# Two constant tables made on the chip from short rows, and two loads in another order

## The chip, the cores and the metric

The kernel runs on one core of one Trainium2 chip. The metric is the device time of one execution in microseconds (us); times are compared by their medians. A core has five engines that run side by side, each through its own queue in order: TensorE (PE in the rows, and PEld for its weight loads), VectorE (DVE), ScalarE (ACT), GpSimd (POOL) and SyncE (SP), which here only issues the loads and stores.

## The reference

Three stages. The first is a decayed linear attention ("retention") over 2 batches, 8 heads, 768 positions, 64 columns; each head has its own decay gamma:

```python
gamma = 1.0 - 2.0 ** (-5.0 - np.arange(H, dtype=np.float32))
for t in range(S):
    state = gamma[None, :, None, None] * state + np.einsum('bhd,bhe->bhde', k[:, :, t], v[:, :, t])
    y[:, :, t] = scale * np.einsum('bhd,bhde->bhe', q[:, :, t], state)
```

Its output, 1536 tokens of 512 columns, goes through two MLPs of width 2048: softplus between the two products of the first, `s * relu(h)**2 + b` between those of the second. Everything is float32.

## The kernel before

**The retention.** Each batch is cut into six chunks of 128 positions, twelve chunks in all; a chunk is done in two *units* of four heads, so unit n is half n % 2 of chunk n // 2. Before a unit stand its *scores* (`att_scores`, line 172: the products of k and q, eight passes on PE) and the *mask* (`att_mask`, line 179: VectorE multiplies the scores by a table). The unit itself (`att_out`, line 191) is, on PE, the product of state and scaled q (not in a batch's first chunk), the product of masked scores and v, and the product of k and scaled v that updates the state. ScalarE and VectorE then take the result out in two parts (`x_hi`, `x_lo`, lines 223 and 229), add up the state (`state`, lines 244 and 246), copy it to where PE reads it (`state_out`, line 255) and decay it (`decay`, line 262). GpSimd makes the scaled v and q of the next chunk (`scale_v`, line 145; `scale_q`, line 157).

**The tables.** They stand in one tile `cst`: `vtab` (128 x 8, decays for v), `gam` (128 x 4, decays for the state), `mask` (128 x 1024: for each head a 128 x 128 triangle of decay powers, divided by the square root of 64) and `gtab` (128 x 512: decay powers for q). All are computed on the host by `_constants` and loaded in two loads, at lines 729 (`vtab`, `gam`, `mask`) and 731 (`gtab`). The masks of scores 0 and 1 need the first, `scale_q(1)` the second.

**The order.** Everything is in an order written out by hand. All loads are issued by SP, one after another, at lines 728 to 738: q and k of chunk 0 (`load_qk`), the mask table, k and v of chunk 0 (`load_kv`), the query table, then q, k and v of the next chunks; `load_next` loads the next 512 KB of MLP weights. Every load of q and k, of k and v, and of weights has 512 KB. Later loads are issued as buffers come free (lines 677 to 680 and 755 to 757).

PE's queue begins with *fill-in products* of zeros that compute nothing (`warm`, line 742): six ahead of score 0 ("first"), three between score 1 and unit 0 ("u0"), one after unit 1 ("s2"). Each is a float32 product of 128 x 128 by 128 columns and shows as two passes. Then come scores 0 and 1, unit 0, unit 1, scores 2 and 3, unit 2, score 4, unit 3, score 5, unit 4, score 6, and so on (line 760). Between the units, `fill` puts steps of the splitting of weights (`split_w`, lines 288 to 303) on VectorE and ScalarE, from unit 3 on.

From unit 8 on, the first MLP's products (`h_mm`, line 354; `acc_mm`, line 405) stand between the units; after the last unit the rest of both MLPs follows, products of 512 columns on PE with the splitting of weights and values into two parts beside them. PSUM banks `ac[2]` and `ac[3]` and the result tiles `xa[0]` and `xa[1]` are free while the retention starts.

Of the kernel before, what the change touches and what calls it, by code (L numbers as in the profile page):

```python
# [10 lines left out]
AF = mybir.ActivationFunctionType  # L11
ALU = mybir.AluOpType

P = 128
B, H, S, D = 2, 8, 768, 64
DM = H * D
DFF = 2048
NT = B * S
C = 128
NC_B = S // C  # L20
NP = H // 2
# [7 lines left out]
RING = 6  # L29
NIN = 4  # L30

WARM = {"first": 6, "u0": 3, "s2": 1}
FIRST, SECOND = (0, 1), (2, 3)
LAG = 3
LAG_U = 3
# [1 line left out]
HF = 2  # L37
HP = NP // HF
# [4 lines left out]
CM = H + NP  # L43
CG = CM + H * C
CW = CG + NP * C


@with_exitstack
def tile_retention_mlps(ctx: ExitStack, tc: tile.TileContext, head, w1, w2, sb, out):
    nc = tc.nc  # L50
# [18 lines left out]
    def bank(pool, tag):  # L69
        return pool.tile([P, 512], F32, tag=tag, name=tag)  # L70

    def sums():

        t = ps_acc.tile([P, 2, 512], F32, tag="acc01", name="acc01")
        return [t[:, 0], t[:, 1], bank(ps_acc, "acc2"), bank(ps_acc, "acc3")], t

    cst = rp.tile([P, CW], F32, tag="cst", name="cst")
    vtab = cst[:, 0:H]
    gam = cst[:, H:CM]
    mask = cst[:, CM:CG].rearrange("p (f h t) -> p f h t", f=HF, h=2)  # L80
    gtab = cst[:, CG:]
# [10 lines left out]
    xa = [cp.tile([P, KC, TT], F32, tag=f"xa{j}", name=f"xa{j}") for j in range(NTILE)]  # L92
# [7 lines left out]
    ac, ac01 = sums()  # L100
# [18 lines left out]
    NCHUNK = B * NC_B  # L119
    NU = NCHUNK * HF  # L120

    consts = head[: P * CW].rearrange("(p x) -> p x", p=P)

    def chunk_of(k):
        at_ = P * (CW + 2 * DM * k)
        return head[at_ : at_ + P * 2 * DM].rearrange("(p x) -> p x", p=P)

    def load_qk(ci):
        t = qk_t[ci] = inp.tile([P, 2, NP, C], F32, tag="qk", name="qk")
        nc.sync.dma_start(out=t.rearrange("p a b t -> p (a b t)"), in_=chunk_of(2 * ci))  # L130

    def load_kv(ci):
        t = kv_t[ci] = inp.tile([P, 2, DM], F32, tag="kv", name="kv")
        nc.sync.dma_start(out=t.rearrange("p a b -> p (a b)"), in_=chunk_of(2 * ci + 1))

    def scale_v(ci):

        if ci % NC_B == NC_B - 1:
            return
        t = scp.tile([P, H, D], F32, tag="v2", name="v2")  # L140
        v = kv_t[ci][:, 1].rearrange("p (h d) -> p h d", h=H)
        vs = vtab.rearrange("p (h o) -> p h o", o=1).to_broadcast([P, H, D])
        cuts = (0, H // 2, H) if ci == 0 else (0, H)
        for a, z in zip(cuts, cuts[1:]):
            nc.gpsimd.tensor_tensor(out=t[:, a:z], in0=v[:, a:z], in1=vs[:, a:z], op=ALU.mult)
        v2_t[ci] = t

    def scale_q(ci):

        if ci % NC_B == 0:  # L150
            return
        t = scp.tile([P, NP, C], F32, tag="q2", name="q2")
        flat = "p a t -> p (a t)"

        cuts = (0, NP // 2, NP) if ci == 1 else (0, NP)
        for a, z in zip(cuts, cuts[1:]):
            nc.gpsimd.tensor_tensor(
                out=t[:, a:z].rearrange(flat), in0=qk_t[ci][:, 0, a:z].rearrange(flat),
                in1=gtab[:, a * C : z * C], op=ALU.mult,
            )  # L160
        q2_t[ci] = t
# [107 lines left out]
    def load_w(w, i):  # L269
        layer, f = divmod(w, NF)  # L270
        t = rawp.tile([P, DM, 2], U32, tag="raw", name="raw")
        nc.sync.dma_start(out=t.rearrange("p a b -> p (a b)"), in_=(w1, w2)[layer][f, :, i].bitcast(U32))
        raw_t[w, i] = t
# [358 lines left out]
    def load_next():  # L632
        x = next(loads, None)
        if x:
            load_w(*x)
# [20 lines left out]
    def unit(n, y, before=lambda: None, mid=lambda: None):  # L656

        att_out(n, y)
        before()
        x_hi(n)  # L660
        mid()
        if n == 1:
            state_out(0)
        if n < N0:
            decay(n - 1)
        state(n)
        if n > 0:
            state_out(n)
        if n >= N0:
            decay(n - 1)  # L670
        x_lo(n)
        ci, f = divmod(n, HF)
        if f == 0 and ci + 1 < NCHUNK:
            scale_q(ci + 1)
            scale_v(ci + 1)
        if f == HF - 1 and ci + NIN < NCHUNK:
            load_qk(ci + NIN)
            if ci == 0:
                load_next()
            load_kv(ci + NIN)  # L680

    def score_to(n, banks):
        while scored[0] < min(n, NU):
            n_, scored[0] = scored[0], scored[0] + 1
            att_scores(n_, banks(n_))
            att_mask(n_, banks(n_))
# [17 lines left out]
    def out_of(y):  # L704
        return y[:, :HC], y[:, HC : HC + HP * D]
# [3 lines left out]
    def fill(n):  # L709

        for _ in range(n):
            if not left[0]:
                if nxt[0] is None or fill.at < slot_free(*nxt[0]):
                    return
                work[0] = split_w(*nxt[0])
                nxt[0] = next(splits, None)
                left[0] = 5
            next(work[0], None)
            left[0] -= 1

    with tc.manual_schedule():
# [3 lines left out]
        nc.vector.memset(st, 0.0)  # L725
        nc.vector.memset(cu[:, 0:1], 0xC0000000)
        nc.vector.memset(cu[:, 1:2], 29)
        load_qk(0)
        nc.sync.dma_start(out=cst[:, :CG], in_=consts[:, :CG])
        load_kv(0)  # L730
        nc.sync.dma_start(out=cst[:, CG:], in_=consts[:, CG:])
        load_qk(1)
        load_kv(1)
        load_qk(2)
        load_next()
        load_kv(2)
        load_qk(3)
        load_kv(3)

        def warm(bank, key):  # L740
            for _ in range(WARM[key]):
                nc.tensor.matmul(bank[:, 0:P], zero[:, 0:P], zero[:, P : 2 * P], start=True, stop=True)

        ys = [bank(ps_h, "h"), bank(ps_y, "y")]
        warm(ac[3], "first")
        scale_q(0)
        scale_v(0)
        score_to(2, lent)
        warm(ac[3], "u0")
        for n in range(N0):  # L750
            if n >= len(ys):
                ys.append(bank(*((ps_h, "h"), (ps_y, "y"))[n % 2]))
            unit(n, out_of(ys[n]))
            if n == 1:
                load_next()
                load_next()
                nc.sync.dma_start(out=sbt, in_=sb)
                warm(ac[3], "s2")

            score_to((2, 4, 5, 6, 7, 8, 9, 10)[n], lent)  # L760
            fill((0, 0, 0, 2, 1, 1, 2, 2)[n])
# [289 lines left out]
        for s in range(S1, NS):  # L1051
            k = s - S1
# [23 lines left out]
        p = PAIRS - 1  # L1076
        for j in (1, 2):
            cuts = (FIRST, SECOND) if j == 1 else (FIRST, SECOND[:1], SECOND[1:])
# [7 lines left out]


def _constants():
    import numpy as np

    gamma = 1.0 - 2.0 ** (-5.0 - np.arange(H, dtype=np.float64))
    t = np.arange(C, dtype=np.float64)
    of = 2 * np.arange(NP)[None, :] + (np.arange(P) >= D)[:, None]
    gap = t[None, :] - t[:, None]

    mask = np.where(gap[:, None] >= 0, gamma[:, None] ** np.maximum(gap, 0)[:, None], 0) / np.sqrt(D)
    mask = mask.reshape(P, HF, HP, 2, C).transpose(0, 1, 3, 2, 4).reshape(P, H * C)
    gtab = gamma[of][:, :, None] ** (t + 1.0)[None, None, :] / np.sqrt(D)
    vtab = gamma[None, :] ** (C - 1.0 - t)[:, None]
    gam = gamma[of] ** C  # L1100
    return np.ascontiguousarray(
        np.concatenate([vtab, gam, mask, gtab.reshape(P, NP * C)], axis=1).astype(np.float32)
    )


def _layout(x):

    v = x.reshape(B, NP, 2, NC_B, C, D)
    return v.transpose(0, 3, 2, 5, 1, 4).reshape(B, NC_B, P, NP, C)


def _natural(x):

    return x.reshape(B, H, NC_B, C, D).transpose(0, 2, 3, 1, 4).reshape(B, NC_B, C, DM)


def _head(q, k, v):

    import numpy as np

    qk = np.stack([_layout(q), _layout(k)], axis=3).reshape(B * NC_B, 1, -1)
    kv = np.stack([_natural(k), _natural(v)], axis=3).reshape(B * NC_B, 1, -1)
    return np.concatenate([_constants().reshape(-1), np.concatenate([qk, kv], axis=1).reshape(-1)])


def _weights(w_in, w_out):
# [33 lines left out]
```

## Time and profile before

| | us |
|---|---|
| median of 3 runs (570.47 to 570.64) | 570.55 |
| profiled execution, its own time | 570.28 |
| its span, first to last instruction | 568.4 |
| PE busy in the span | 561.8 |
| VectorE busy | 408.1 |
| GpSimd busy | 341.8 |
| ScalarE busy | 339.1 |
| moved by DMA | 50.58 MB |

The profile is of one execution; its times count from the first instruction, and 1.9 us of the device time lie outside the span. Busy time of PE is from the start of a pass to a modelled end, so PE can be busy and still not at its peak. A group of a row is the engine, the line of the kernel, what is written and read, and the number of instructions. The work that ended last before an engine could go on is named behind `<-`.

### The profile page before, as it was taken

What the parts mean: (1) busy time and instruction counts of PE and PEld (TensorE: products, weight loads), DVE (VectorE), ACT (ScalarE), POOL (GpSimd) and SP (SyncE); (2) the same over time, 40 slices, a digit from 0 to 9 for tenths busy, and PEclk for the clock granted to TensorE, in tenths of its full rate; (3) what the DMA queues carried; (4) which work ended last, traced back from release to release, by engine and by line L of the source; (5) the groups of instructions that cost most, each with busy time, mean ns of one, the idle gap of its engine ahead of it and who ended that gap; (6) DMA issues with size and microseconds to landing.
All of it is one profiled execution on the core that took longest, in us unless ns stands there. A gap on an engine that the chain in (4) does not pass through costs nothing.

```text
span 568.4 us, 8119 instructions
## 1 busy us (share of the span) xinstructions
PE 561.8 (99%) x2968; PEld 460.9 (81%) x2968; DVE 408.1 (72%) x619; ACT 339.1 (60%) x616; POOL 341.8 (60%) x286
## 2 busy tenths in 40 slices
PE   8999999999999999999999999999999999999997
PEld 7787888888878878888888888888888888888885
DVE  4898778876777968997878876765766757655233
ACT  3756663545565565543427788768586866666560
POOL 3456657777589696843515996646565646556130
PEclk9999999999999999999999999999999999999999
DMA  8996121202221212322121122121222121100005
GB/s 330 415 349 221 39 76 37 75 1 76 71 77 37 80 52 93 110 91 97 39 74 39 36 90 97 40 78 69 75 76 74 51 99 37 38 0 1 0 18 205
DMA packets 14870, 50.58 MB, mean 89 GB/s; under 512 B 1776, under 2 KB 1776, under 8 KB 14832
## 3 DMA queue, kind: packets, MB, share of 16 engines
q1 hardware_dynamic: 14832, 50.08, 25.4%
q8 instruction: 23, 0.38, 0.3%
q14 instruction: 15, 0.12, 0.1%
HBM read 46.93 MB, written 3.15 MB: 88 GB/s over the span
## 4 chain that ended last, share of the span: by engine, by line
PE 90%; DMA 3%; POOL 3%; DVE 2%; ACT 1%; issue 1%; SPq 0%; DVEq 0%; POOLq 0%
PE acc L581 32%; PE acc L405 12%; PE h L495 9%; PE h L354 8%; PE y L503 6%; PE third L503 6%; PE y L495 4%; PE y L354 4%; PE third L495 2%; DMA qk<-head 2%; PE h L503 2%; PE y L191 2%; PE s L172 1%; PE h L191 1%; POOL c L555 1%
## 5 line engine op out<-in xcount | busy, mean ns | idle before, releaser
L591 DVE TENSOR_TENSOR xa<-acc,xa 128x512 f32<-128x512 f32 x132 | 82.4, 684 | 86.0 <-PE acc L581 85.9
L115 POOL TENSOR_TENSOR wl<-wm,wh 128x512 fp32r<-128x512 f32 x64 | 83.8, 1310 | 95.1 <-ACT wh L112 93.5
L115 POOL TENSOR_TENSOR gl<-c,gh 128x512 fp32r<-128x512 f32 x69 | 91.7, 1332 | 82.0 <-ACT gh L112 61.8
L581 PE MATMUL acc<-wh,gh 128*128 128x512 f32 x192 | 74.9, 390 | 0.0
L581 PE MATMUL acc<-wh,gl 128*128 128x512 f32 x192 | 74.8, 390 | 0.0
L112 ACT ACTIVATE gh<-c 128x512 fp32r<-128x512 f32 x69 | 43.7, 633 | 15.7 <-POOL c L555 11.7
L581 PE MATMUL acc<-wl,gh 128*128 128x512 f32 x192 | 52.5, 389 | 0.0
L295 ACT ACTIVATE wm<-raw 128x512 f32<-128x512 f32 x64 | 42.3, 661 | 7.1 <-POOL wl L115 7.0
L581 PEld LDWEIGHTS acc<-wh,gh 128*128 128x128 f32 x192 | 36.0, 188 | 8.2 <-DVE xa L591 0.4
L112 ACT ACTIVATE wh<-wm 128x512 fp32r<-128x512 f32 x64 | 39.7, 621 | 4.6 <-DVE wm L303 4.6
L292 DVE SCALAR_TENSOR_TENSOR word<-raw,cu,word 128x512 uint32<-128x512 uint32 x54 | 40.8, 756 | 1.9
L581 PEld LDWEIGHTS acc<-wl,gh 128*128 128x128 f32 x192 | 36.0, 188 | 7.5
L581 PEld LDWEIGHTS acc<-wh,gl 128*128 128x128 f32 x192 | 36.0, 188 | 7.4
L303 DVE SCALAR_TENSOR_TENSOR wm<-wm,word 128x512 f32<-128x512 f32 x54 | 37.1, 688 | 6.1 <-ACT wm L295 1.2
L297 DVE SCALAR_TENSOR_TENSOR word<-raw,cu,word 128x512 uint32<-128x512 uint32 x54 | 40.5, 751 | 0.8
L553 ACT ACTIVATE c<-c,sbt 128x512 f32<-128x512 f32 x48 | 39.2, 817 | 1.6
L527 ACT ACTIVATE c<-c 128x512 f32<-128x512 f32 x21 | 13.3, 633 | 43.2 <-DVE c L520 42.3
L405 PE MATMUL acc<-gh,wh 128*128 128x512 f32 x96 | 38.2, 398 | 0.1
L367 ACT ACTIVATE t<-t 128x512 f32<-128x512 f32 x24 | 15.1, 629 | 38.8 <-DVE t L361 38.7
L581 PE MATMUL acc<-gl,wh 128*128 128x512 f32 x96 | 37.8, 394 | 0.0
L581 PE MATMUL acc<-gh,wh 128*128 128x512 f32 x96 | 37.8, 393 | 0.0
L405 PE MATMUL acc<-gl,wh 128*128 128x512 f32 x96 | 37.5, 391 | 0.0
(230 smaller groups left out, 1427.7 us busy)
## 6 DMA issues: line engine op xcount, KB each, us to landing
raw<-w SPq DMA_DIRECT2D x64, 512.0 KB, 3.5
qk<-head SPq DMA_DIRECT2D x12, 512.0 KB, 8.1
kv<-head SPq DMA_DIRECT2D x12, 512.0 KB, 8.1
out<-xa SPq DMA_DIRECT2D x12, 256.0 KB, 2.1
cst<-head SPq DMA_DIRECT2D x1, 518.0 KB, 4.4
cst<-head SPq DMA_DIRECT2D x1, 256.0 KB, 5.4
sbt<-sb SPq DMA_DIRECT2D x1, 1.0 KB, 10.2
```

Of the source, the lines that this page charges most:

```text
L112: nc.scalar.activation(hi, src, AF.Copy)
L115: lo_eng.tensor_tensor(out=lo, in0=src, in1=hi.bitcast(F32), op=ALU.subtract)
L292: nc.vector.scalar_tensor_tensor(out=x, in0=hw, scalar=cu[:, 0:1], in1=x, op0=ALU.bitwise_and, op1=ALU.bitwise_or)
L295: nc.scalar.activation(m, hw.bitcast(F32), AF.Square)
L297: nc.vector.scalar_tensor_tensor(out=x, in0=lw, scalar=cu[:, 1:2], in1=x, op0=ALU.logical_shift_right, op1=ALU.bitwise_or)
L354: nc.tensor.matmul(ps, w[:, cc * P : (cc + 1) * P], r[j][:, cc, :], start=i == 0, stop=i == len(ops) - 1)
L405: nc.tensor.matmul(acc_t[la, g, j][cc], *ops[i], start=f4 == 0 and i == 0, stop=ends(s) and i == 2)
L495: nc.tensor.matmul(ps, w[a][:, k * P : (k + 1) * P], x[b][:, k], start=start and i == 0, stop=i == len(ops) - 1, skip_group_check=True,)
L503: nc.tensor.matmul(ps, w[a][:, k * P : (k + 1) * P], (xh, xl)[b][j][:, k], start=i == 0, stop=i == len(ops) - 1)
L553: nc.scalar.activation(c, c, AF.Identity, scale=sbt[:, 0:1], bias=sbt[:, 1:2])
L581: nc.tensor.matmul(acc_t[la, p, "pair", j][cc], *ops[i], start=half == 0 and i == 0, stop=half == 1 and i == 2)
L591: nc.vector.tensor_tensor(out=dst, in0=ps, in1=dst, op=ALU.add)
```

## The change

The two loads of tables go. In their place stand two small loads ahead of all others. One brings four rows of 1920 numbers into the first four partitions of `xa[0]`; the other brings `vtab`, `gam` and one 128 x 128 triangle of ones (`upper`) into `xa[1]`. Each half of the mask table is then made on PE as a product of 4 x 128 by 4 x 512 (row k has gamma to the power -t of one head; the other operand has gamma to the power t, in that head's 128 columns only), and VectorE multiplies it by the triangle into `mask`. The query table is a product of 2 x 128 by 2 x 512, copied by ScalarE into `gtab`. VectorE copies `vtab` and `gam` into `cst`.

Of the fill-in products, three stay ahead of the tables and the other seven go. `load_qk(3)` is issued ahead of the first `load_next`. `scale_v` is cut in two halves for chunk 1 too.

```diff
-WARM = {"first": 6, "u0": 3, "s2": 1}
+WARM = 3
+NROW, CT = 4, CM + C
+RW = 2 * (C + DM) + P + NP * C
...
-        cuts = (0, H // 2, H) if ci == 0 else (0, H)
+        cuts = (0, H // 2, H) if ci < 2 else (0, H)
...
+        rows = xa[0].rearrange("p a b -> p (a b)")[:NROW, :RW]
+        upper = xa[1][:, 0, CM : CM + C]
+        nc.sync.dma_start(out=rows, in_=head[: NROW * RW].rearrange("(p x) -> p x", p=NROW))
+        tab = head[NROW * RW : NROW * RW + P * CT].rearrange("(p x) -> p x", p=P)
+        nc.sync.dma_start(out=xa[1].rearrange("p a b -> p (a b)")[:, :CT], in_=tab)
         load_qk(0)
-        nc.sync.dma_start(out=cst[:, :CG], in_=consts[:, :CG])
         load_kv(0)
-        nc.sync.dma_start(out=cst[:, CG:], in_=consts[:, CG:])
         load_qk(1)
         load_kv(1)
         load_qk(2)
-        load_next()
         load_kv(2)
         load_qk(3)
+        load_next()
         load_kv(3)
...
+        def tables():
+            at_ = 0
+            for f, to in ((0, ac[3]), (1, ys[1])):
+                l, r = rows[:, at_ : at_ + C], rows[:, at_ + C : at_ + C + DM]
+                nc.tensor.matmul(to, l, r, start=True, stop=True)
+                nc.vector.tensor_tensor(
+                    out=mask[:, f].rearrange("p h (i t) -> p (h i) t", i=HP), in0=to.rearrange("p (k t) -> p k t", t=C),
+                    in1=upper.rearrange("p (o t) -> p o t", o=1).to_broadcast([P, 2 * HP, C]), op=ALU.mult,
+                )
+                at_ += C + DM
+            nc.vector.tensor_copy(cst[:, :CM], xa[1][:, 0, :CM])
+
+        def query_table():
+            at_ = 2 * (C + DM)
+            l, r = rows[:2, at_ : at_ + P], rows[:2, at_ + P :]
+            nc.tensor.matmul(ac[2], l, r, start=True, stop=True)
+            nc.scalar.activation(gtab, ac[2], AF.Copy)
+
         ys = [bank(ps_h, "h"), bank(ps_y, "y")]
-        warm(ac[3], "first")
+        warm(ac[3])
+        tables()
         scale_q(0)
         scale_v(0)
         score_to(2, lent)
-        warm(ac[3], "u0")
+        query_table()
         for n in range(N0):
...
-                warm(ac[3], "s2")
```

## Rows read from the trace of the kernel before

**Rows 1.** Stretches: length; PE, PEld, DVE, ACT, POOL busy (instructions); PEclk, DMA share, GB/s.

```profile
16.00:18.00 2.00, 1.11 (x16) 0.99 (x18) 1.63 (x4) 1.47 (x5) 0.99 (x1) 1.00 1.03 422
18.00:560.00 542.00, 541.74 (x2765) 444.06 (x2762) 395.62 (x593) 330.31 (x591) 334.75 (x275) 1.00 0.23 79
```

**Rows 2.** Chain that ended last, its pieces: start us, us, what.

```profile
1.17 4.39 DMA cst<-head
...
5.58 11.27 DMA qk<-head
...
36.40 2.96 PE h L354 x12
...
39.38 0.70 DVE t L361
...
47.27 3.03 PE acc L405 x12
```

**Rows 3.** Timeline of PE, 0 to 17 us: start us, us, engine, line, what, count.

```profile
1.45 2.93 PE L742 MATMUL acc<-xa 128*128 128x128 f32 x12 [1.45 <-DVE xa L724]
4.36 1.22 PE L172 MATMUL s<-qk 64*128 64x128 f32 x8
...
6.37 0.99 PE L742 MATMUL acc<-xa 128*128 128x128 f32 x6
7.29 0.66 PE L191 MATMUL h<-a,kv 128*64 128x128 f32 x8
...
8.78 0.49 PE L742 MATMUL acc<-xa 128*128 128x128 f32 x2
9.20 0.71 PE L172 MATMUL s<-qk 64*128 64x128 f32 x8
...
10.29 0.66 PE L191 MATMUL h<-q,st 128*64 128x128 f32 x8
10.78 0.61 PE L191 MATMUL h<-a,kv 128*64 128x128 f32 x8
...
11.72 0.72 PE L172 MATMUL s<-qk 64*128 64x128 f32 x8
12.37 0.66 PE L191 MATMUL y<-q,st 128*64 128x128 f32 x8
...
13.62 0.72 PE L172 MATMUL acc<-qk 64*128 64x128 f32 x8
...
16.89 0.71 PE L172 MATMUL s<-qk 64*128 64x128 f32 x8 [0.94 <-DMA qk<-head]
```

**Rows 4.** Timeline of SP, the issues of three loads.

```profile
0.74 0.38 SPq L130 DMA_DIRECT2D qk<-head  x1
...
4.11 0.45 SPq L272 DMA_DIRECT2D raw<-w  x1
...
5.58 0.33 SPq L130 DMA_DIRECT2D qk<-head  x1
```

**Rows 5.** Landings of the first and second load of rows 4: KB, us from issue.

```profile
qk<-head SPq DMA_DIRECT2D x1, 512.0 KB, 3.6
raw<-w SPq DMA_DIRECT2D x1, 512.0 KB, 8.9
```

**Rows 6.** Timeline of VectorE: masks of scores 0 and 2, first weights step.

```profile
5.66 0.69 DVE L179 TENSOR_TENSOR a<-s,cst 128x512 f32<-128x512 f32 x1 [3.71 <-PE s L172]
...
9.96 0.69 DVE L179 TENSOR_TENSOR a<-s,cst 128x512 f32<-128x512 f32 x1
...
15.29 0.68 DVE L288 TENSOR_SCALAR acc<-raw 128x512 uint32<-128x512 uint32 x1
```

**Rows 7.** Line 742, all fill-in passes: duration ns min/median/max.

```profile
L742 PE MATMUL acc<-xa x20: 275/421/582, 1.5 to 9.0; 128*128 128x128 f32 x20
```

**Rows 8.** Page, costliest groups: busy us, mean ns of one.

```profile
L112 ACT ACTIVATE gh<-c 128x512 fp32r<-128x512 f32 x69 | 43.7, 633 | 15.7 <-POOL c L555 11.7
```

**Rows 9.** Timeline of GpSimd, q of chunk 1.

```profile
8.88 1.41 POOL L157 TENSOR_TENSOR q<-qk,cst 128x256 f32<-128x256 f32 x2 [0.74 <-DMA qk<-head]
```

More of the change, by code (lines that the diff above doesn't have):

```diff
@@ L120, in tile_retention_mlps @@
     NU = NCHUNK * HF
-    consts = head[: P * CW].rearrange("(p x) -> p x", p=P)
     def chunk_of(k):
-        at_ = P * (CW + 2 * DM * k)
+        at_ = NROW * RW + P * (CT + 2 * DM * k)
         return head[at_ : at_ + P * 2 * DM].rearrange("(p x) -> p x", p=P)
@@ L734, in tile_retention_mlps, with warm @@
         load_qk(2)
-        load_next()
         load_kv(2)
         load_qk(3)
+        load_next()
         load_kv(3)
-        def warm(bank, key):
-            for _ in range(WARM[key]):
+        def warm(bank):
+            for _ in range(WARM):
                 nc.tensor.matmul(bank[:, 0:P], zero[:, 0:P], zero[:, P : 2 * P], start=True, stop=True)
+        def tables():
[14 more added lines that the diff above has]
+            nc.scalar.activation(gtab, ac[2], AF.Copy)
         ys = [bank(ps_h, "h"), bank(ps_y, "y")]
-        warm(ac[3], "first")
+        warm(ac[3])
+        tables()
         scale_q(0)
@@ L1093, in _constants @@
     of = 2 * np.arange(NP)[None, :] + (np.arange(P) >= D)[:, None]
[L1094 to L1098, printed above, removed]
+    rows = np.zeros((NROW, RW))
+    at_ = 0
+    for f in range(HF):
+        for k in range(2 * HP):
+            h, i = divmod(k, HP)
+            g = gamma[2 * (f * HP + i) + h]
+            rows[k, at_ : at_ + C] = g**-t
+            rows[k, at_ + C + k * C : at_ + C + (k + 1) * C] = g**t / np.sqrt(D)
+        at_ += C + DM
+    for h in range(2):
+        rows[h, at_ + h * D : at_ + (h + 1) * D] = 1
+        rows[h, at_ + P :] = (gamma[h::2, None] ** (t + 1.0) / np.sqrt(D)).reshape(-1)
     vtab = gamma[None, :] ** (C - 1.0 - t)[:, None]
     gam = gamma[of] ** C
-    return np.ascontiguousarray(
-        np.concatenate([vtab, gam, mask, gtab.reshape(P, NP * C)], axis=1).astype(np.float32)
-    )
+    upper = t[None, :] >= t[:, None]
+    tab = np.concatenate([vtab, gam, upper], axis=1)
+    return np.concatenate([rows.reshape(-1), tab.reshape(-1)]).astype(np.float32)
 def _layout(x):
@@ L1122, in _head @@
     kv = np.stack([_natural(k), _natural(v)], axis=3).reshape(B * NC_B, 1, -1)
-    return np.concatenate([_constants().reshape(-1), np.concatenate([qk, kv], axis=1).reshape(-1)])
+    return np.concatenate([_constants(), np.concatenate([qk, kv], axis=1).reshape(-1)])
 def _weights(w_in, w_out):
```

## The prediction

> **What bounds the kernel now.** I read the table of stretches first. TensorE (PE) is busy for 541.74 of the 542.00 us from 18 to 560 us, and for 1.11 of the 2.00 us from 16 to 18, where the DMA engines stand at a share of 1.03 and 422 GB/s [rows 1]. What the change can win must therefore come before 17 us, or be taken out of PE's own work, and the change takes nothing out of it later on.
>
> The chain of waits, read next, says what the start hangs on: the load of the mask table, issued at 1.17 and landed 4.39 us later, then the load of the fourth chunk's q and k, issued at 5.58 and landed 11.27 later at 16.85, then PE [rows 2]. In PE's timeline this is the 0.94 us of waiting ahead of the scores at 16.89 [rows 3]. It is the only long hole after 1.45 us. Two things hide smaller ones: the three fill-in products at 6.37 and the one at 8.78, which compute nothing that is used. So the start is a race between loads and PE. I take 16.89, the start of score 6, as the mark: whatever it moves by, all later PE work moves by, since from there PE is full.
>
> Between 39.36 and 47.27 the chain runs through VectorE and ScalarE and not PE [rows 2]; its first step, at 39.38, is released by a PE product, so it moves with PE too.
>
> **The loads.** The removed table has 128 x (12 + 1024 + 512) floats, 793 KB. In its place come 4 x 1920 floats (31 KB) and 128 x 140 floats (72 KB). That is 690 KB less, and at 416 GB/s (estimate, from the 422 GB/s of [rows 1] less a little for the slower first us) 1.7 us less of a queue that is full. The fourth chunk's q and k also pass the first weights on the SP queue, one 524 KB load, 1.26 us. They land 2.9 us earlier, at about 13.9; the weights land at 4.11 + 8.9 = 13.0 now [rows 4, 5], and 1.7 earlier plus 1.26 later gives 12.6. VectorE first touches them at 15.29 [rows 6], so that move costs nothing while unit 3's work stands ahead of it. On the other side, two issues now stand ahead of chunk 0's q and k on the SP queue: its issue goes from 0.74 to about 1.64 (0.33 to 0.45 each and a short pause, [rows 4]), and its landing from 4.34 [rows 4, 5] to at most 5.24. Every other load stands in the same order behind it.
>
> **The new head of the chain.** On PE's queue the order becomes: 3 warming products, two table products (4 rows by 512 columns, float32), scores 0 and 1, the query-table product, unit 0. The first table product waits for the rows, and everything named behind it waits with it. On VectorE two multiplies by the triangle and a copy of 12 columns come ahead of the masks of scores 0 and 1; on GpSimd scale_v(0) waits for that copy; on ScalarE one copy of 128x512 makes the query table, and GpSimd's scale_q(1) waits for it.
>
> - Rows landed: the first load of before takes 3.6 us from issue [rows 5], of which 1.26 are its bytes. So 0.74 + 2.34 = 3.1 and a little for 31 KB: 3.3. Bounds: 3.1 and, if small rows are slow, 3.8.
> - One table product: the fill-in products are float32 of 128 columns in two passes. Twelve passes take 2.93 us in all and the last lasts 0.42 [rows 3, 7], so a pass starts every 0.21 to 0.23; from 6.37 on six take 0.99 and the last 0.28, so 0.11 to 0.14. 512 columns are four times that and two passes: 1.7 us at the lower speed, 0.9 at the higher.
> - Which speed: the granted clock reads 1.00 in the stretches, but by the spacing PE runs at the lower of its two levels (1.2 GHz) until after the scores of 4.36 (1.22 us for eight passes against 0.71 at 16.89) and at 2.4 GHz from 6.37 [rows 3]. Ahead of that it had worked since 1.45 with one gap of 0.2. I take the rise at 6.4 again. The two table products then run from 3.3 almost wholly at the low level: 3.4 us, less 0.2 for the piece after 6.4, to 6.5.
> - Scores 0 and 1 at the high level: 10.29 - 9.20 = 1.09 [rows 3], to 7.6. Query-table product: 0.9, to 8.5.
> - Does VectorE hold it up? The second product is out at about 6.7; multiply 0.69 (as the masks, [rows 6]), copy 0.1 (estimate, no like row; at most the 0.69 of a whole multiply), mask 0.69: 8.2. No. GpSimd: first half of v after 7.5, needed 0.4 into unit 0. No.
>
> So **unit 0 starts at 8.6** (with a little for hand-over) instead of 7.29 [rows 3].
>
> **From unit 0 to score 6**, all durations from [rows 3]: units 0 and 1, 8.78 - 7.29 = 1.49; the fill-in at 8.78 is gone; scores 2 and 3, 1.09; unit 2, 1.25 as unit 3 (12.37 to 13.62; unit 2 itself took 1.43 with a wait for v); score 4, 0.65; unit 3, 1.25; score 5, 0.65; unit 4, 1.25. Sum 7.63. What comes late next is mask 2: it ended at 9.96 + 0.69 = 10.65 [rows 6], 1.87 after the end of unit 1, held by VectorE's work on unit 1 and not by PE. Unit 2's second part would now be wanted 1.09 + 0.49 = 1.58 after it; with 0.13 of hand-over it waits 0.42. The fill-in that was removed had covered exactly this: its 0.42 turns into a wait. Score 6: 8.6 + 7.63 + 0.42 = **16.65**. GpSimd keeps up: query table at 8.5 + 0.2 + 0.63 [rows 8] = 9.3, two halves of q in 1.41 [rows 9] give the first at 10.0 and unit 2 wants it at 11.2. The load that ended the chain (13.9) is now 2.7 us early.
>
> Before: 16.89. Gain 0.24 us, of the 1.7 us that the loads give back; the table products on PE at the lower clock take the rest. The profiled execution took 570.28 (span 568.4), 0.27 under the median of 570.55; 570.28 - 0.24 = 570.04, on the median's scale **570.3**. Differences under 0.2%, 1.1 us, are about what a measurement here cannot tell from nothing.
>
> A rule that speaks against the form of the new load: the Trainium skill, "DMA: Bandwidth & Descriptors", section "Why a DMA increments its semaphore by 16 and not by 1", says that a transfer is spread over the largest number of engines up to 16 that divides its slowest dimension, so four rows use four engines. No load of this trace has four rows. By it the 31 KB would take 0.3 us and not 0.08, and the rows would land 0.2 later; by the sum that is 570.4 and not 570.3.
>
> **The rivals.**
> 1. *The clock stays low through the head (slower).* In before, PE had nearly no gap from 1.45 on; now three warming products end at about 2.8 and PE then stands still until the rows land, and after that it streams four-row operands, which no row here shows raising the clock. If it is still low: tables to 3.3 + 3.4 = 6.7, scores 2.0 (4.36 to 6.37), query table 1.7, unit 0 at 10.4, score 6 at 18.4: +1.5, **572.1**. If units 0 and 1 and the next scores (2.6 us) run at the low level too, up to 574.5. It is slower by the bound from unit 0 at 10.0 on. For it: the gap is new; against it: the fill before has gaps of 0.2 to 0.4 and rose on time. The Trainium skill, "TensorE: Matmul & The Clock Gate", section "What's actually happening", says that the lower clock is the default and activity releases it; that agrees with rows 3, and says nothing of four-row products.
> 2. *The loads count in full (faster).* If the clock is already high when the table products run (one profiled execution shows one time of the rise), they take 1.8 us: tables to 5.1, scores 6.2, query table 7.1, masks on VectorE ready at about 7.0; unit 0 at 7.2 and score 6 at 15.2: **568.9**. Against it: PE's work starts no earlier than before, so nothing says that the clock rises sooner.
> 3. *The start moves and the end does not.* With the hole ahead of 16.89 gone, VectorE has its weights work (15.29, [rows 6]) and the masks in less time, runs late against PE, and the 0.24 is given back where VectorE leads the chain, from 39.38 on [rows 2]: **570.5**. Against it: that piece waits for PE first.
>
> **Chances.** Forecast 0.60 (its own range 569.7 to 571.0, from rows landing between 3.1 and 3.8 and the clock's rise half a us either way); rival 1, 0.20; rival 2, 0.13; rival 3, 0.07. Faster by over 1.1 us: rival 2 nearly whole and a little of the forecast, 0.15. Slower: most of rival 1 and a little of the forecast, 0.18. Same: 0.67. The range takes in rival 2 and rival 1's first price: 568.8 to 572.1.
>
> **What would show it.** Right: PE's table products start at 3.1 to 3.8 and take about 1.7 each; unit 0 starts at 8.3 to 9.0; no wait of PE for a load after 9 us; a wait of about 0.4 in unit 2, and score 6 at about 16.6. Wrong: products of 0.9 each (rival 2), scores 0 and 1 still at 1.2 us for eight passes (rival 1), a PE wait for q2 or v on GpSimd, a wait for a load near 14 us, or the loss or gain showing after 18 us.

## The result, and the profile after

| | before | after |
|---|---|---|
| median of 6 executions each, us | 570.51 | 574.33 |
| range | 570.44 to 570.64 | 573.79 to 574.68 |
| profiled execution / its span | 570.28 / 568.4 | 573.91 / 572.0 |

After over before is 1.0065 (95% interval 1.0052 to 1.0078): 3.8 us slower. Such a ratio, here and below, is taken over all executions, so it need not be the ratio of the two medians. The forecast was 570.3, with 572.1 as the upper end.

PE's timeline of the changed kernel, which answers to rows 3 (`...` marks rows left out):

```profile
1.45 1.65 PE L745 MATMUL acc<-xa 128*128 128x128 f32 x6 [1.45 <-DVE xa L724]
3.18 2.07 PE L752 MATMUL acc<-xa 4*128 4x512 f32 x2
5.05 1.91 PE L752 MATMUL y<-xa 4*128 4x512 f32 x2
6.89 1.23 PE L172 MATMUL s<-qk 64*128 64x128 f32 x8
...
8.90 2.07 PE L763 MATMUL acc<-xa 2*128 2x512 f32 x2
10.90 1.12 PE L191 MATMUL h<-a,kv 128*64 128x128 f32 x8
...
13.65 1.23 PE L172 MATMUL s<-qk 64*128 64x128 f32 x8
14.67 0.96 PE L172 MATMUL acc<-qk 64*128 64x128 f32 x8
15.56 0.66 PE L191 MATMUL h<-q,st 128*64 128x128 f32 x8
...
16.82 0.72 PE L172 MATMUL s<-qk 64*128 64x128 f32 x8
...
20.61 0.72 PE L172 MATMUL s<-qk 64*128 64x128 f32 x8
```

Eight passes of scores tell the clock: 1.23 us at 6.89 and still 1.23 at 13.65, 0.72 at 16.82. So the clock rises in the scores of 14.67 and not at 6.4. The clock events stored with the two traces say the same: the first grant of full speed comes at 15.40 us, and at 6.52 in the kernel before. Unit 0 starts at 10.90 and not 7.29. Score 6, the mark, starts at 20.61 and not 16.89: 3.72 later, against 3.63 in the two profiled executions. The whole loss therefore lies ahead of the mark. Its two halves: 3.61 ahead of unit 0; from unit 0 to score 6 9.71 us against 9.60. In that second stretch the low clock costs (13.65 - 10.90) - 1.49 = 1.26 in units 0 and 1 and (15.56 - 13.65) - 1.09 = 0.82 in scores 2 and 3, and nearly as much is won back: the wait of 0.94 ahead of score 6, the fill-in of 0.42, and the waits for v.

The table of stretches, which answers to rows 1 (length; PE, PEld, DVE, ACT, POOL busy; PEclk; DMA share, GB/s):

```profile
6.00:14.00 8.00, 8.00 (x54) 5.27 (x54) 2.78 (x6) 1.21 (x3) 3.50 (x6) 1.00 1.01 393
16.00:18.00 2.00, 2.00 (x38) 1.81 (x36) 1.03 (x4) 1.04 (x4) 0.45 (x1) 1.00 1.02 418
18.00:560.00 542.00, 541.73 (x2813) 444.42 (x2808) 397.01 (x597) 334.54 (x604) 335.67 (x275) 1.00 0.23 77
```

The hole from 16 to 18 is closed. PE is busy for the 8.00 us from 6 to 14 with 54 passes, and the PEclk column reads 1.00 there although the passes run at half speed: the column knows the stored clock events alone, and none stands ahead of the first rise. From 18 us on PE is as full as before.

The chain of waits, which answers to rows 2, has one load left, the new rows:

```profile
0.74 2.40 DMA xa<-head
3.14 0.04 issue
3.18 2.07 PE acc L752 x2
...
43.08 0.70 DVE t L361
```

From 3.18 to 43.06 it is a chain on PE alone. The step of VectorE at 39.38 stands at 43.08, 3.70 later: it moved with PE.

VectorE's rows, which answer to rows 6:

```profile
5.29 0.69 DVE L753 TENSOR_TENSOR cst<-acc,xa 128x512 f32<-128x512 f32 x1 [3.34 <-PE acc L752]
7.00 0.69 DVE L753 TENSOR_TENSOR cst<-y,xa 128x512 f32<-128x512 f32 x1 [1.01 <-PE y L752]
...
8.16 0.69 DVE L179 TENSOR_TENSOR a<-s,cst 128x512 f32<-128x512 f32 x1 [0.39 <-PE s L172]
```

The multiplies take the 0.69 that was assumed; VectorE waits for PE in front of each, and behind 1.45 us PE waits for nothing that VectorE makes here.

### The profile page after: what moved, and what is told of

Read it like the earlier page. It is cut to its first block, busy times and chain, and to the rows that moved or that the text cites. A ratio compares the mean times of both kernels' runs of the same rounds, so it can differ in the third digit from the quotient of the medians.

```text
span 572.0 us, 8111 instructions
## 1 busy us (share of the span) xinstructions
PE 566.5 (99%) x2960; PEld 462.5 (81%) x2960; DVE 409.4 (72%) x622; ACT 339.8 (59%) x617; POOL 341.8 (60%) x287
## 4 chain that ended last, share of the span: by engine, by line
PE 93%; POOL 3%; DVE 2%; ACT 1%; issue 1%; DMA 0%; DVEq 0%; POOLq 0%
PE acc L581 32%; PE acc L405 12%; PE h L495 9%; PE h L354 7%; PE y L503 6%; PE third L503 6%; PE y L495 4%; PE y L354 4%; PE y L191 2%; PE third L495 2%; PE h L503 2%; PE s L172 2%; PE h L191 2%; PE acc L172 1%; POOL c L555 1%
## 5 line engine op out<-in xcount | busy, mean ns | idle before, releaser
L367 ACT ACTIVATE t<-t 128x512 f32<-128x512 f32 x24 | 15.1, 628 | 38.6 <-DVE t L361 38.5
```

## The experiments

The theory after this result, **R**: products that read few rows (partitions) do not raise TensorE's clock, so the changed head of the kernel stays at the low level until units 0 and 1 have run. The rivals: **G**, the new gap ahead of the first table product (its weight load waits 0.4 us for the rows) delays the rise; **L**, the long passes of 512 columns with few weight loads do. Medians are given beside those of the kernel before on the same chip.

**Rows alone, in the kernel before.**

```diff
-                nc.tensor.matmul(bank[:, 0:P], zero[:, 0:P], zero[:, P : 2 * P], start=True, stop=True)
+                nc.tensor.matmul(bank[:, 0:P], zero[:4, 0:P], zero[:4, P : 2 * P], start=True, stop=True)
```

> The kernel before with one edit: all fill-in products read 4 of the 128 partitions. Their number, place and columns stay. Theory R (products of few rows do not raise TensorE's clock): the passes stay at the lower spacing (0.21 us) past 9 us, units 0 and 1 take 1.3 us each and not 0.75, time 571.0 to 573.0. Rival G (what delays the clock in the changed kernel is the gap ahead of its first table product): there is no new gap here, so the spacing falls to 0.11 at 6.4 as before and the time is 570.5. Rival L (the long passes of 512 columns with few weight loads delay it): as G, 570.5.

Measured: 572.97 against 570.44 (ratio 1.0034, 1.0022 to 1.0047). Seven executions lie from 572.8 to 573.8 and three from 570.9 to 571.1. PE's timeline of one of the seven:

```profile
4.66 1.23 PE L172 MATMUL s<-qk 64*128 64x128 f32 x8 [0.29 <-DMA qk<-head]
5.68 1.06 PE L172 MATMUL acc<-qk 64*128 64x128 f32 x8
6.67 1.64 PE L742 MATMUL acc<-xa 4*128 4x128 f32 x6
8.24 1.12 PE L191 MATMUL h<-a,kv 128*64 128x128 f32 x8
...
11.72 1.22 PE L172 MATMUL s<-qk 64*128 64x128 f32 x8
...
16.06 0.83 PE L172 MATMUL s<-qk 64*128 64x128 f32 x8
```

No table product, no long pass, and no new gap in the fill-in: the rows read are the edit. The fill-in at 6.67 takes 1.64 where it took 0.99 [rows 3], and the scores are still at 1.22 at 11.72; the first clock event is at 16.34. R's account holds in this execution, and by the times in the other six, some a little over its 573.0; G and L predicted 570.5. The three quick executions say that the rise is not at one time in all executions, and that few rows do not hold it back in every one.

**The gap closed, in the changed kernel.** Six fill-in products ahead of the tables (`WARM = 6`).

> The changed kernel with six fill-in products ahead of the tables and not three: PE has no gap from 1.45 until the table products, which start at 4.2 and not 3.18. Theory R: the clock rises as late as in the changed kernel (near 15), everything 1.0 us later: 575.0 to 575.5. Rival G: it rises near 6.4, in the middle of the tables: unit 0 at 9.1, 570.8 to 571.3. Rival L: as R.

Measured: 574.29 against 570.44 (1.0055, 1.0027 to 1.0084); two of five executions at 571.3 and 571.6, three at 574.3 to 575.3. In a profile of the latter the first table product stands right behind the fill-in, and the scores at 14.78 still take 1.23:

```profile
4.31 2.07 PE L752 MATMUL acc<-xa 4*128 4x512 f32 x2
...
14.78 1.23 PE L172 MATMUL s<-qk 64*128 64x128 f32 x8
```

So the rise is late without the gap too, in three of five; two of these three are at the 575.2 to 575.3 that R named. The two quick ones are near what G named. All six executions of the changed kernel were late, so closing the gap may have changed the odds; with five and six executions that is not shown.

**The same products, 4 rows and 128.** Both kernels set the row tile to zero first and bridge the wait with eight fill-in products; the second lets the table products read all partitions:

```diff
-                l, r = rows[:, at_ : at_ + C], rows[:, at_ + C : at_ + C + DM]
+                l, r = flat[:, at_ : at_ + C], flat[:, at_ + C : at_ + C + DM]
...
-            l, r = rows[:2, at_ : at_ + P], rows[:2, at_ + P :]
+            l, r = flat[:, at_ : at_ + P], flat[:, at_ + P : RW]
```

> The changed kernel with the row tile set to zero ahead of its load, which therefore is issued near 2.3 us, and eight fill-in products to bridge the wait; table products still read 4 rows (2 for the query table). Control of the next kernel. Theory R: clock rises after 10 us, unit 0 near 12.5, 574.5 to 576.5. Rival G: no gap, so it rises near 6.5, 571.4. Rival L: as R.

> As the control with zeroed rows, with one difference: the table products read all 128 partitions (124 of them zero), same columns, same passes. Theory R: the clock rises near 6.5, tables done near 7.6, unit 0 at 9.7 and score 6 at 17.8, so 571.0 to 571.8, 3 to 5 us under the control. Rival G: same as the control. Rival L (long passes): same as the control, both late.

Measured: 575.79 with 4 rows (three of four at 575.8 to 576.0, one at 573.17), **571.28** with 128 (ten, 570.41 to 571.76); 1.0084 and 1.0012 of the kernel before. PE's timeline with 4 rows, then with 128:

```profile
5.21 2.04 PE L755 MATMUL acc<-xa 4*128 4x512 f32 x2
7.05 1.91 PE L755 MATMUL y<-xa 4*128 4x512 f32 x2
8.89 1.23 PE L172 MATMUL s<-qk 64*128 64x128 f32 x8
...
12.90 1.12 PE L191 MATMUL h<-a,kv 128*64 128x128 f32 x8
```

```profile
5.32 1.28 PE L755 MATMUL acc<-xa 128*128 128x512 f32 x2
6.44 1.02 PE L755 MATMUL y<-xa 128*128 128x512 f32 x2
7.39 0.72 PE L172 MATMUL s<-qk 64*128 64x128 f32 x8
...
8.48 1.13 PE L766 MATMUL acc<-xa 128*128 128x512 f32 x2
9.54 0.66 PE L191 MATMUL h<-a,kv 128*64 128x128 f32 x8
...
17.45 0.72 PE L172 MATMUL s<-qk 64*128 64x128 f32 x8
```

Same columns, same passes, as many weight loads, and 4.5 us between them: that excludes L, and shows in the changed kernel itself that the rows decide. The first clock event is at 17.50 with 4 rows and at 5.71 with 128. The latter is only 0.4 us into the table products, behind fill-in that both kernels have alike, so one such pair of profiles could be the chance of the moment; the reading rests on all executions, of which none with 128 rows is as slow as the quickest with 4.

The edits change the rows of both operands at once: which of the two matters, and where between 4 rows and the 64 of the scores the line lies, was not tested.

At the high clock a table product takes 0.95 to 1.1 (0.9 was the forecast's price), unit 0 stands at 9.54 and the mark at 17.45.

**Work of many rows ahead of the tables.** Seven fill-in products, then scores 0 and 1, then the tables, then the two masks.

```diff
-        tables()
-        scale_q(0)
-        scale_v(0)
-        score_to(2, lent)
+        for n in range(2):
+            att_scores(n, lent(n))
+        tables()
+        scale_q(0)
+        scale_v(0)
+        for n in range(2):
+            att_mask(n, lent(n))
+        scored[0] = 2
```

> The changed kernel with seven fill-in products of 128 rows and then scores 0 and 1 ahead of the tables, and the masks of these scores behind them: the work ahead of the tables is of many rows up to 6.4. Theory R: the clock is high from 6.4 on, tables 6.5 to 8.4 at 0.9 each, unit 0 near 9.4 to 10.0, score 6 near 17.6, time 571.0 to 571.6. If the table products themselves keep or bring the low clock: 574 to 575.

Measured: 573.15 against 570.54 (1.0055, 1.0039 to 1.0071), between the two times named. In the profile (575.63, the slowest of four) PE waits 0.89 for q and k of chunk 0 ahead of the scores at 5.70, the tables begin at 7.71 with the clock still low, and 5.4 us of products of 4 and 2 rows follow. The clock was not up before the few-row work began, so this execution did not test what the kernel was made for. The other three (572.74 to 573.40) may have: their mean granted clock is 0.994 to 0.996, where every execution of the kernel before has 0.998 or more. A mean counts a fall only behind a first rise, so in these three the clock had risen and fell again; where it fell is not shown.

**A gap with full rows, in the kernel before** (`"first": 3`).

> The kernel before with three fill-in products ahead of score 0 and not six: PE stands still from about 2.8 us until q and k of chunk 0 land near 4.4, a gap of 1.6 us, three times that of the changed kernel; every product still reads 64 or 128 rows. Theory R alone (rows, not gaps): the clock rises by 7 us and the time is 570.4 to 570.8. If a gap ahead of the rise delays it too (rival G as a second cause): units 0 and 1 at the low level, 571.0 to 573.0 in some or all executions.

Measured: 570.40 against 570.52 (0.9999, 0.9990 to 1.0009): no difference. But in the profile the fill-in at 6.37 takes 1.65 and unit 0 1.12; by the scores at 10.60 (0.72) the clock is high:

```profile
4.35 1.23 PE L172 MATMUL s<-qk 64*128 64x128 f32 x8 [1.25 <-DMA qk<-head]
...
6.37 1.65 PE L742 MATMUL acc<-xa 128*128 128x128 f32 x6
...
10.60 0.72 PE L172 MATMUL s<-qk 64*128 64x128 f32 x8
```

So behind a gap of 1.25 us the rise came 3 us later in this execution (first clock event at 9.55 and not 6.52), and not 9. The kernel before hides that behind its loads: score 6 stands at 16.75. As the rise is not at one time in all executions, one of them does not show that the gap is the reason, here or with the 0.9 of the kernel above.

**What the loads are worth.** Tables neither loaded nor made (the output lacks masks and decays), loads in the new order, fill-in as before.

```diff
-        nc.sync.dma_start(out=cst[:, :CG], in_=consts[:, :CG])
+        nc.gpsimd.memset(cst, 0.1)
...
-        nc.sync.dma_start(out=cst[:, CG:], in_=consts[:, CG:])
```

> What the loads could give at most: as the kernel with the loads in the new order, but no table is loaded or made; the table tile is filled with a constant by GpSimd, so the output is not the reference's (masks and decays are left out). Fill-in products as before, so unit 0 stays at 7.3 and the clock rises near 6.4. By the prediction's sum score 6 at 15.3, 1.5 us earlier: 569.0. If the stall only moves to VectorE or ScalarE: 569.5 to 570.5.

Measured: 568.97 against 570.54 (0.9972, 0.9960 to 0.9983), 1.57 us. In the profile unit 0 stands at 6.80 and score 6 at 14.85, both 0.5 earlier than named, because the clock rises earlier in this execution (at 5.12). Between them lie 8.05 us without a wait for a load, which is the sum's 7.63 and the 0.42 of the fill-in. So with no load in the way PE goes at the pace of the sum. How early the loads of the changed kernel land is another question: there two small loads stand ahead of all others.

**The order alone.** The kernel before, with the first weights behind k and v of chunk 2 and q and k of chunk 3.

> The kernel before with one part of the change alone: k and v of chunk 2 and q and k of chunk 3 are loaded ahead of the first weights; tables still loaded, all fill-in products kept. If the load at 16.85 was the only thing that held score 6, and PE the only thing after it, score 6 starts near 15.7 and the time falls by 0.9 to 1.2: 569.3 to 569.6. If VectorE (weights work, masks) or GpSimd gives it back: 570.0 to 570.5.

Measured: 570.11 against 570.54 (0.9992, 0.9983 to 1.0000), 0.4 us. The mark moves by 1.14, and 0.7 of that is given back. PE's and VectorE's rows:

```profile
15.75 0.71 PE L172 MATMUL s<-qk 64*128 64x128 f32 x8
22.79 0.50 PE L354 MATMUL h<-xh,wh 128*128 128x512 f32 x1 [0.30 <-ACT wh L112]
```

```profile
16.22 0.69 DVE L288 TENSOR_SCALAR acc<-raw 128x512 uint32<-128x512 uint32 x1 [0.62 <-DMA raw<-w]
```

VectorE now waits for the weights, its first step is at 16.22 instead of 15.29, and PE's first MLP product waits for what comes of it; that product stands at 22.79, against 23.23 before. The move is not free once the start is quick.

**Only the query table on the chip.** The mask table is loaded; one product of 2 rows takes the place of the three fill-in products ahead of unit 0. The loads stand in the new order and `scale_v` is in halves for chunk 1, as in the change. A second version reads 128 rows, 126 of them set to zero by GpSimd; a third loads the first weights ahead of q and k of chunk 3 again.

```diff
-        nc.sync.dma_start(out=cst[:, CG:], in_=consts[:, CG:])
+        nc.sync.dma_start(out=rows, in_=head[P * CG : P * CG + 2 * RW].rearrange("(p x) -> p x", p=2))
...
-        warm(ac[3], "u0")
+        nc.tensor.matmul(ac[2], rows[:, :P], rows[:, P:], start=True, stop=True)
+        nc.scalar.activation(gtab, ac[2], AF.Copy)
```

> A cut of the change that puts little on PE: mask table loaded as before, only the query table made on the chip, by a product of 2 rows that stands where the three fill-in products ahead of unit 0 stood; loads in the new order, v of chunk 1 scaled in halves. The product takes 0.9 at the high clock, as long as the fill-ins; the loads are 0.6 us shorter. Score 6 near 15.4: 569.0 to 569.4. If the two-row product comes before the rise of the clock it delays it: 571 or more in those executions.

> As the kernel that makes only the query table on the chip, with one difference: its product reads 128 partitions, of which GpSimd has set 126 to zero ahead of the load of the two rows. Theory R: the clock no longer falls after the product and does not rise late, so the slow executions (571 to 572) go: 569.2 to 569.9 in all of them, under the kernel before. If the spread of the two-row version came from something else (the landing of k and v of chunk 0, which came 1 us late in its profile): 569.4 to 572 again.

> As the kernel with the query table from a product of 128 rows, but the first weights are loaded ahead of q and k of chunk 3 (k and v of chunk 2 still ahead of both). If what takes the rest of the gain back is the late landing of the first weights (16.3 there, PE's first MLP product then waits for them): weights near 15, the wait goes, 569.2 to 569.6. If q and k of chunk 3 then hold score 6 again: 569.9 to 570.3, no gain.

Measured: 570.70 (569.42 to 572.34) with 2 rows, **569.89** (569.24 to 570.18) with 128, 569.84 (569.18 to 570.32) with the weights earlier; 1.0002, 0.9989 (0.9980 to 0.9998) and 0.9988 (0.9979 to 0.9997) of the kernel before. Stretches and PE's timeline of the 2-row version:

```profile
6.00:9.00 3.00, 2.22 (x24) 1.15 (x24) 0.87 (x2) 0.60 (x1) 1.08 (x2) 1.00 1.01 392
9.00:12.50 3.50, 3.50 (x36) 3.16 (x32) 1.66 (x5) 2.36 (x8) 3.40 (x6) 0.51 1.03 423
```

```profile
6.04 1.12 PE L751 MATMUL acc<-xa 2*128 2x512 f32 x2
7.92 0.66 PE L192 MATMUL h<-a,kv 128*64 128x128 f32 x8 [0.77 <-DMA kv<-head]
...
10.81 1.23 PE L173 MATMUL s<-qk 64*128 64x128 f32 x8
```

Here the clock is high at 6.04 and at 7.92 (0.66), and then falls: granted 0.51 from 9 to 12.5, behind a product of 2 rows and a wait of 0.77. This profile also shows how to read the spacing: the scores at 10.81 take 1.23 where 0.51 is granted, the time that they take ahead of the first rise.

The mean granted clock tells the twelve executions apart: five have 0.999 or 1.000 and take 569.42 to 570.01, five have 0.996 or 0.997, a fall as in this profile, and take 570.46 to 571.49; the two slowest (572.25 and 572.34) have 1.000, which fits a late first rise. With 128 rows, in whose profile PE waits 0.65 at the same place, all have 0.998 or more, and none takes over 570.32. R had named 569.2 to 569.9, and four of the eleven executions of the second version lie above that, at 570.13 to 570.18.

The two versions with 128 rows have the lowest medians of this study with a complete output, 0.6 to 0.7 us under the kernel before. Loading the weights earlier takes away PE's wait for them (its first MLP product moves from 22.87 to 22.24) and changes the median by 0.05, which is within its uncertainty; where that went stays open.

## Why the prediction was wrong

- **What bounds the start, and that PE is full behind the mark: right.** Mark 3.72 later, end 3.63 later, PE busy for 541.73 of 542.00 us behind 18.
- **Rows landed at 3.3: right** (3.14). By the Trainium skill, "DMA: Bandwidth & Descriptors", section "Why a DMA increments its semaphore by 16 and not by 1", four rows use four engines. The trace agrees: the load is four packets of 7,680 bytes side by side, from 1.67 to 2.12. But the landing, 2.40 after issue, shows no sign of the 0.2 that this was to cost.
- **Price of a table product at the low clock, 1.7: near** (3.18 to 5.05 and 5.05 to 6.89, 1.85 each). VectorE and GpSimd do not hold up the head: right. The sum had scores 0 and 1 and the query-table product at the high clock, 1.09 and 0.9; at the low one they took 2.01 and 2.00.
- **"I take the rise at 6.4 again": this is the step that failed.** The text had in front of it that the rise came after 128-row and 64-row products, and that none of the rows showed four-row products raising the clock; it took the rise over as a time. It is not one. In the changed kernel PE was at work without a gap from 3.18 on and the rise came at 15.4. This put unit 0 at 10.90 and not at 8.6, and units 0 and 1 and the scores behind them ran at the low clock too. Rival 1 with its second price (up to 574.5) is what happened: 574.33. Its first price had unit 0 at 10.4 and score 6 at 18.4; measured are 10.90 and 20.61. The mechanism had been named and was given 0.20, and the range was closed at its first price, 572.1, though its own reason, that no row shows four-row products raising the clock, leads to the second: the first work of 128 rows behind the tables is units 0 and 1 themselves.
- The Trainium skill, "TensorE: Matmul & The Clock Gate", section "What's actually happening", was cited for the low clock as default and activity as its release. The rows agree with that (1.23, then 0.72). In the profiled execution of the kernel before with fill-in on 4 rows, the first twelve passes take 2.92 us as against 2.93, and the clock rises at 16.34 and not at 6.52.
- **"That move costs nothing": wrong, and hidden.** The weights were to land at 12.6; in the changed kernel they land at 5.25 + 9.7 = 14.95. There VectorE comes to them at 20.39 only, so nothing waits. In the kernel with the order alone the same move gives back 0.7. The sum moved them behind one load, 1.26; the edit moves them behind two, k and v of chunk 2 and q and k of chunk 3, so 2.5.
- **The loads' 1.7 us: wrong for the changed kernel, and hidden too.** Up to q and k of chunk 2 the loads of q, k and v stand in the same order in both kernels. The q and k of chunk 2 landed at 3.59 + 7.6 = 11.2 before and at 3.47 + 7.3 = 10.8 after, 0.4 earlier:

```profile
3.59 0.48 SPq L130 DMA_DIRECT2D qk<-head  x1
qk<-head SPq DMA_DIRECT2D x1, 512.0 KB, 7.6
```

```profile
3.47 0.48 SPq L130 DMA_DIRECT2D qk<-head  x1
qk<-head SPq DMA_DIRECT2D x1, 512.0 KB, 7.3
...
5.25 0.45 SPq L272 DMA_DIRECT2D raw<-w  x1
raw<-w SPq DMA_DIRECT2D x1, 512.0 KB, 9.7
```

  The two small loads put the landing of q and k of chunk 0 from 4.34 to 1.58 + 4.0 = 5.58, 1.24 later; the sum named such a delay (0.9) for that load and did not take it off the 1.7 for those behind it. With both terms as measured the weights come to 13.0 - 0.4 + 2.5 = 15.1, near the 14.95. PE waited for no load, so this cost no time here; the 1.57 us of the kernel without tables has no small loads ahead and does not show the 1.7 for this one.
- **The wait in unit 2 in place of the fill-in:** not seen in the changed kernel, where the low clock left VectorE time; with 128 rows PE's second part of unit 2 starts 0.72 behind the first and not 0.49 (12.12 to 12.84), 0.23 of the 0.42.
- With the clock up, the forecast's mark of 16.65 would still have asked for rows at 3.3. The version with 128 rows issued their load 2 us later (at 2.69), its first table product starts at 5.32, its mark is at 17.45 and its time 0.8 over before. What the changed kernel would take with four-row products at the high clock was not measured.

## What to carry to other kernels

Work that is put on TensorE at the start of a kernel is paid at the clock that this work itself earns, so list for each product how many rows it reads before taking a speed for it, and read the clock from the spacing of passes. A small product on few rows is cheap in bytes and dear in time; padding its operands with zero rows added no passes here and took 4.5 us off, though setting the rows to zero first put their load 2 us later. When a load is moved behind another, look for the next reader of the one that lost, in a kernel in which the start is as quick as you hope.

## What the hardware showed

- Products of 4 rows, back to back for 3.7 us and then mixed with scores, left TensorE at its low level (1.2 GHz) until 15.4 us in the changed kernel; where the same passes read 128 rows, it was at the high level (2.4 GHz) from 5.7 us on in the profiled execution.
- The clock can fall again within a busy start: 0.51 granted for 3.5 us, in the version with one product of 2 rows, behind that product and a wait of 0.77. By their mean granted clock, 0.994 to 0.996, the quick executions of the changed kernel with more fill-in ahead of its 4-row products had a fall too.
- The time of the rise differs between executions of one kernel, by enough to make two groups: 570.9 to 571.1 and 572.8 to 573.8 (the kernel before with fill-in on 4 rows), 571.3 to 571.6 and 574.3 to 575.3 (the changed kernel with six fill-in products ahead of the tables). A profile shows one of them.
- The PEclk column reads 1.00 ahead of the first rise, where the passes run at half speed (1.23 us for eight passes of scores, as where 0.51 is granted).

```profile
L742 PEld LDWEIGHTS acc<-xa x20: 186/333/338, 1.4 to 8.9; 128*128 128x128 f32 x20
```

This row of line 742 in the kernel before (min, median, max ns) shows both levels for one form: weight loads of 186 and of 338 ns.
